# Products with v of two neighbouring groups issued together in a fused attention and MLP kernel

## The chip, the cores and the metric

The kernel runs on one core of one Trainium2 chip. The metric is the device time of one launch in microseconds (us). A comparison of two kernels here can tell them apart from about 0.3% on. TensorE (PE in the rows, its weight loads PEld), VectorE (DVE), ScalarE (ACT), GpSimd (POOL) and SyncE (SP, which issues the DMAs here) run side by side and wait for each other by semaphores.

## The reference

Attention with two kinds of masks over 8 batches, 8 heads, 576 tokens and 64 elements per head, then a token mix of low rank and an MLP with a residual:

```python
scores = q @ k.T / sqrt(64)
# heads 0..3: the last 32 tokens; heads 4..7: every 4th of the last 128
scores = where(mask, scores, -1e9)
attn = softmax(scores)
x = (attn @ v) -> [batch, token, 512]
h = x.T @ U @ V               # rank 32, over the tokens
u = x + h.T
out = u + relu(u @ w_ch1) @ w_ch2     # 512 -> 2048 -> 512
```

## The kernel before, in words

**Attention.** Because of the masks, 64 query rows need only 96 keys. A batch has 18 tiles of 64 query rows by four heads (for heads 4 to 7 the tokens are put in an order in which every 4th token is a neighbour). Two tiles make a **group**, so there are 9 groups per batch (NGB) and 72 in all; a group has four units of two heads each. For a group `score` (L375, L386) makes the scores s, `soften` masks them and takes the exponent (L403 to L410) into the tile p, `turn` (L436, L439; L423 in the early groups) transposes p into one of the buffers `pts`, and `weighted` multiplies it with v (L449) into a PSUM tile pv and divides by the row sums (L453, L454, L479). The sum comes from a column of ones beside v. One group's product with v is 16 matmuls in the trace (8 in the program; each fp32 product is executed as two), with 96 rows and 64 columns of the array in use, where the MLP's have 128 and 128.

**Where the result goes.** For heads 0 to 3, L479 writes x directly. For heads 4 to 7 it writes a tile xp, which from the third batch on has a single buffer, and DMAs (L483) carry its rows to x in the plain token order. Groups 0 to 3 of a batch are of heads 0 to 3 alone, group 4 is half and half, groups 5 to 8 are of heads 4 to 7.

**Token mix.** `split_x`, `t_mm` (L519, tile t) and `mix` (L543, tile m, added to x in L545) do the part with U and V, in 5 pieces of a batch's tokens; one of the 5 has 64 rows, and its matmuls t use 64 rows of the array, the others 128.

**MLP.** Chunks of 384 tokens: `layer1` (L742, tile ph, 12 matmuls for each of 16 columns f) and `layer2` (L759, tile acc, 9 matmuls). For every f, hh (ACT, L747) and hl (DVE, L748) bring ph to SBUF as two halves. The order is layer1(f), layer2(f - 1), so hl of f is read after layer1(f + 1).

**What sets the order.** `batch_items` lists the work of a batch's attention as steps s: `pre` (loads of v and `weighted` of group s - 2, LAG = 2), the four units of group s, and `post` (`turn`). From batch 2 on (SPLIT) each of these has a due time of its own, and the MLP's loop calls what is due between its matmuls (`slot`). Below that, a list scheduler orders the instructions of each engine by its own estimate of time; the order on an engine is fixed at build time. PSUM tiles of the tag "ps" (s, pv, t, m, tp) share three buffers, and the v tiles of the later batches (two per group) three.

Names in the rows: qk, qkr and qks are queries with keys (loaded, split in two halves), vs is V, us is U, w1h, w1l, w2h, w2l the weights' halves.

Of the kernel before, what the change touches and what calls it, by code (L numbers as in the profile page):

```python
# [10 lines left out]
F32 = mybir.dt.float32  # L11
# [15 lines left out]
P = 128  # L27
QB = 64
NJ = S // QB
KB = QB + WIN  # L30
# [10 lines left out]
UNITS = 4  # L41
QK1 = P + KB
DV = D + 1
PV = 2 * DV
# [3 lines left out]
SPLIT = 2  # L48
TILES = [(0, j) for j in range(NJ)] + [(1, NJ - 1)] + [(1, j) for j in range(NJ - 1)]
NGB = len(TILES) // 2  # L50
# [3 lines left out]
LAG = 2  # L54
# [33 lines left out]
F_LAST = 13  # L88
RAWS = 4
VS = 4  # L90
QKS = 9
XPS = 4
DVE_FROM = 2
# [57 lines left out]
def attention_moe_kernel(ctx: ExitStack, tc: tile.TileContext, qk1, qk2, vv, masks, wide, ident, ut, vt, w1, w2, out):  # L151
    nc = tc.nc

    const = ctx.enter_context(tc.tile_pool(name="const", bufs=1))
    work = ctx.enter_context(tc.tile_pool(name="work", bufs=2))
    xpool = ctx.enter_context(tc.tile_pool(name="xpool", bufs=NX))
    dram = ctx.enter_context(tc.tile_pool(name="dram", bufs=2, space=bass.MemoryType.DRAM))
    psum = ctx.enter_context(tc.tile_pool(name="psum", bufs=3, space=bass.MemoryType.PSUM))
# [19 lines left out]
    us = const.tile([P, 9, 2 * RANK], F32R, name="us")  # L178
    vs = const.tile([P, P + S], F32R, name="vs")
    signs = [const.tile([P, DM, 2], F16, name=f"sign{i}") for i in range(NSIGN)]  # L180
    NPT = 2
    pts = [const.tile([KB, UNITS, P], F32, name=f"pt{i}") for i in range(NPT)]
    for p in pts:
        nc.gpsimd.memset(p, 0.0)
# [112 lines left out]
    loaded = {}  # L297
# [7 lines left out]
    def load_v(g, i):  # L305
        if (g, 1, i) not in loaded:
            us_ = slice(2 * i, 2 * i + 2)
            if g < NGB:
                if i == 0:
                    t = xpool.tile([P, UNITS, PV], F32, tag="x", name=f"v{g}")[0:KB]  # L310
                    nc.sync.dma_start(out=t, in_=vv[g])
                    loaded[g, 1, 0] = t[:, 0:2]
                    loaded[g, 1, 1] = t[:, 2:4]
            else:
                t = work.tile([KB, 2, PV], F32, tag="v", name=f"v{g}_{i}", bufs=3)
                nc.sync.dma_start(out=t, in_=vv[g][:, us_])
                loaded[g, 1, i] = t

# [99 lines left out]
    def turn(g, p_sb):  # L418
        pt = pts[g % NPT]
        if g < PE_T:  # L420
# [18 lines left out]
                    nc.vector.transpose(out=pt[ks, :, rs], in_=p_sb[rs, :, ks])  # L439
        return pt  # L440

    def weighted(g, pt):
        b = g // NGB
        pv = psum.tile([P, UNITS, DV], F32, tag="ps", name=f"pv{g}")
        for u in range(UNITS):
            v_sb = loaded[g, 1, u // 2]
            for h in range(2):
                hs = slice(h * DV, (h + 1) * DV)
                nc.tensor.matmul(pv[QB * h:QB * (h + 1), u, :], lhsT=pt[:, u, QB * h:QB * (h + 1)],  # L449
                                 rhs=v_sb[:, u % 2, hs], start=True, stop=True)  # L450
        pool, n_ = (early, 3) if g < NGB else (work, 2)
        ssum = pool.tile([P, UNITS], F32, tag="ssum", name=f"ssum{g}", bufs=n_)
        nc.vector.tensor_scalar(out=ssum, in0=pv[:, :, D], scalar1=1e-9, scalar2=None, op0=ALU.add)  # L453
        nc.vector.reciprocal(out=ssum, in_=ssum)  # L454
        moves = []
        xp = None
        for i in range(2):
            half, j = tile_of(g, 2 * i)
            us_ = slice(2 * i, 2 * i + 2)
            cs = slice(half * HALF_D, (half + 1) * HALF_D)  # L460
            if half == 0:
                t, row = divmod(b * S + j * QB, P)
                dst = x_tile(t)[row:row + QB, cs]
            else:
                if xp is None:
                    if b == 0:
                        xp = early.tile([P, HALF_D], F32, tag="xp", name=f"xp{g}", bufs=XPS)
                    elif b < SPLIT and g % 2:
                        xp = spare[:, 0:HALF_D]
                    else:  # L470
                        xp = work.tile([P, HALF_D], F32, tag="xp", name=f"xp{g}", bufs=1)
                    part = next(p for p, js in enumerate(DPART) if j in js)
                row = QB * DPART[part].index(j)
                dst = xp[row:row + QB]
                moves += [(t, to, n, row + r) for r, t, to, n in runs_of(b, half, j)]
            dst4 = dst.rearrange("p (u h d) -> p u h d", u=2, h=2)
            for h in range(2):
                rs = slice(QB * h, QB * (h + 1))
                nc.vector.tensor_tensor(  # L479
                    out=dst4[:, :, h, :], in0=pv[rs, us_, 0:D],  # L480
                    in1=ssum[rs, us_].unsqueeze(2).broadcast_to([QB, 2, D]), op=ALU.mult)
        for t, to, n, r in sorted(moves):
            nc.sync.dma_start(out=x_tile(t)[to:to + DIL * (n - 1) + 1:DIL, HALF_D:], in_=xp[r:r + n])  # L483
        if moves and b == 0:
            split(b, part, 1, xp, slice(0, QB * len(DPART[part])))
# [96 lines left out]
    def batch_items(b):  # L582
        held = {}
        turned = set()
        attn = []
        for s in range(NGB + LAG):
            g = NGB * b + s

            def pre(s=s, g=g):
                if 0 < s <= NGB:  # L590
                    load_v(g - 1, 0)
                if s >= LAG:
                    weighted(g - LAG, held.pop(g - LAG))
                if b > 0 and 0 < s <= NGB:
                    load_v(g - 1, 1)

            def post(s=s, g=g):
                late = g - (NGB * b < PE_T)
                if late in state and late not in turned:
                    turned.add(late)  # L600
                    held[late] = turn(late, state.pop(late)[0])

            def some(us, g=g):
                for u in us:
                    score(g, u)
                for u in us:
                    n = UNITS * g + u
                    if n >= N2:
                        split_qk(n + LOOK)
                        fetch(n + LOOK + DMA_LOOK)  # L610
                    elif n >= UNITS * NE and n % 2 and n + 2 * TB - 1 < N2:
                        fetch(n + 2 * TB - 1)
                for u in us:
                    soften(g, u)

            step = UNITS if b < SPLIT else STEP
            units = [lambda us=range(u, u + step), some=some: some(us) for u in range(0, UNITS if s < NGB else 0, step)]
            if b < SPLIT:
                attn.append([lambda pre=pre, units=units, post=post: (pre(), [x() for x in units], post())])
            else:  # L620
                attn.append([pre] + units + [post])
        n = len(batch_parts(b))
        after = []
        for c in range(2):
            more = []
            for i in range(n + 1):
                def go(i=i, c=c):
                    if i > 0:
                        t_mm(b, i - 1, c)
                    if i < n and (b, c) != (0, 1):  # L630
                        split_x(b, i, c)
                more.append(go)
            more.append(lambda c=c: t_evict(b, c))
            more += [lambda i=i, c=c: mix(b, i, c) for i in range(n)]
            after.append(more)
        first = NJ // 2 + LAG + 1 + (POST0 if b == 0 else 0)
        per = -(-len(after[0]) // (len(attn) - first))
        if b >= SPLIT:
            timed = []
            for i, step in enumerate(attn):  # L640
                timed += [(i, step[0])] + [(i + UNIT0 + (UNIT1 - UNIT0) * u / len(step[1:-1]), x) for u, x in enumerate(step[1:-1])] + [(i + POST_AT, step[-1])]
                if i >= first:
                    k = (i - first) * per
                    timed += [(i + (m + 0.5) / per, x) for m, x in enumerate(after[0][k:k + per])]
            timed += [(len(attn) + m * TAIL, x) for m, x in enumerate(after[1])]
            end = len(attn) + len(after[1]) * TAIL
            return [(t / end, x) for t, x in sorted(timed, key=lambda e: e[0])]
        items = [x for step in attn[:first] for x in step]
        rest = attn[first:]
        if b == 0:  # L650
            hold = after[0][n + 1:]
            after[0] = after[0][:n + 1]
            m = n + 1
            mixes = [x for p in zip(hold[1:], after[1][m + 1:]) for x in p]
            turns = [lambda t=t: transp(t) for t in range(CT)]
            cut = 2 * CT
            after[1] = [hold[0]] + after[1][:m + 1] + mixes[:cut] + turns + mixes[cut:]
        per = -(-len(after[0]) // len(rest))
        for i, it in enumerate(rest):
            items += it  # L660
            items += after[0][i * per:(i + 1) * per]
        items += after[1]
        return [(i / len(items), x) for i, x in enumerate(items)]
# [60 lines left out]
    for c in range(NCHUNK):  # L724
# [56 lines left out]
        for i in range(CT):  # L781
            t = c * CT + i
# [82 lines left out]
```

## Time and profile before

| | |
|---|---|
| median of 3 runs | 1025.01 us (1024.31 to 1027.09) |
| profiled execution, its own time | 1021.92 us |
| its span in the trace | 1020.1 us |
| PE busy | 982.4 us (96%) in 5904 matmuls |
| DVE busy | 625.1 us (61%) |
| ACT busy | 411.2 us (40%) |
| POOL busy | 324.2 us (32%) |
| share of the chain that ended last: PE | 87% |
| groups' products with v (L449) in that chain | 4% |

The profiled execution is 3.1 us below the median. Busy time of PE is an upper view: matmuls are pipelined, and a row's length overlaps the next one's. What a matmul costs the stream is the step from its start to the next start, and such steps are read from the timeline. The chain of waits tells which engine ended each wait on the path to the last instruction.

### The profile page before, as it was taken

The page shows a single profiled execution, that of the slowest core. Times are in us where ns is not written, and L with a number is a line of the kernel's source. Part 1 is how long each engine was busy: PE and PEld are TensorE (multiplying, and loading weights), DVE is VectorE, ACT ScalarE, POOL GpSimd, SP SyncE. Part 2 cuts the span into 40 slices and gives each one's busy share as a digit, 9 for nine tenths or more (in the row PEclk, how much of TensorE's full clock was granted, in tenths as well). Part 3 has the DMA queues.
Part 4 walks back from the last instruction along what each step waited for, and adds up shares of the span by engine and source line. Part 5 has one row for each costly group of instructions (what it writes and reads, how often), then busy time and mean ns, then how long its engine had stood idle before and what let it go on. Part 6 is the DMA issues. An engine that isn't in the chain of part 4 may idle for free.

```text
span 1020.1 us, 18204 instructions
## 1 busy us (share of the span) xinstructions
PE 982.4 (96%) x5904; PEld 861.3 (84%) x5904; DVE 625.1 (61%) x2155; ACT 411.2 (40%) x986; POOL 324.2 (32%) x519
## 2 busy tenths in 40 slices
PE   7479998999999999999999999999999999999998
PEld 6268886888888888888898888888888888899997
DVE  5978667777368754876457873777647864411211
ACT  3889874343244423445233532434323442111110
POOL 0668673252143421344131621425313431000000
PEclk9579997999999999999999999999999999999999
DMA  9578544243332423333242432434332420400000
GB/s 296 179 238 255 166 143 127 63 129 86 87 88 83 120 73 80 112 111 96 69 107 79 127 81 58 134 83 121 93 80 81 122 61 25 134 1 1 32 1 31
DMA packets 96910, 103.31 MB, mean 101 GB/s; under 512 B 12816, under 2 KB 83536, under 8 KB 96816
## 3 DMA queue, kind: packets, MB, share of 16 engines
q1 hardware_dynamic: 96816, 102.16, 35.0%
q8 instruction: 47, 0.77, 0.3%
q14 instruction: 47, 0.39, 0.1%
HBM read 80.08 MB, written 17.30 MB: 95 GB/s over the span
## 4 chain that ended last, share of the span: by engine, by line
PE 87%; DMA 5%; DVE 3%; ACT 2%; SPq 1%; issue 1%; POOL 0%; DVEq 0%; ACTq 0%; POOLq 0%
PE ph L742 38%; PE acc L759 38%; PE pv L449 4%; PE s L375 3%; PE t L519 2%; PE s L386 1%; DMA zd<-z 1%; DMA raw<-ut 1%; PE m L543 1%; DMA qk<-qk 1%; SPq L483 1%; DMA x<-xp 1%; DMA qkr<-qk 1%; DMA v<-vv 1%; DMA raw<-w 0%
## 5 line engine op out<-in xcount | busy, mean ns | idle before, releaser
L759 PE MATMUL acc<-w2h,hh 128*128 128x512 f32 x576 | 229.0, 398 | 1.1 <-DVE x L784 1.1
L759 PE MATMUL acc<-w2l,hh 128*128 128x512 f32 x576 | 228.0, 396 | 0.0
L352 POOL TENSOR_TENSOR qks<-qkr,qks 128x160 fp32r<-128x160 f32 x192 | 103.6, 539 | 378.5 <-ACT qks L351 238.0
L748 DVE SCALAR_TENSOR_TENSOR hl<-ph,hh 128x384 fp32r<-128x384 f32 x192 | 106.4, 554 | 177.8 <-ACT hh L747 176.5
L759 PE MATMUL acc<-w2h,hl 128*128 128x512 f32 x576 | 210.9, 398 | 0.0
L747 ACT ACTIVATE hh<-ph 128x384 fp32r<-128x384 f32 x192 | 93.8, 488 | 265.0 <-PE ph L742 241.2
L742 PE MATMUL ph<-uth,w1l 128*128 128x384 f32 x768 | 176.2, 341 | 0.0
L742 PE MATMUL ph<-uth,w1h 128*128 128x384 f32 x768 | 173.8, 342 | 0.4 <-ACT uth L579 0.3
L742 PE MATMUL ph<-utl,w1h 128*128 128x384 f32 x768 | 173.0, 339 | 0.0
L410 ACT ACTIVATE p<-p,nmax 128x160 f32<-128x160 f32 (+1 forms) x288 | 111.4, 410 | 122.7 <-DVE nmax L406 119.2
L742 PEld LDWEIGHTS ph<-uth,w1h 128*128 128x128 f32 x768 | 140.1, 190 | 16.7 <-ACT uth L579 1.4
L742 PEld LDWEIGHTS ph<-uth,w1l 128*128 128x128 f32 x768 | 137.4, 190 | 1.1 <-issue 0.4
L742 PEld LDWEIGHTS ph<-utl,w1h 128*128 128x128 f32 x768 | 135.1, 188 | 1.6 <-DVE utl L580 0.2
L351 ACT CAST qks<-qkr 128x288 fp32r<-128x288 f32 x192 | 80.8, 430 | 124.7 <-PE s L375 87.8
L759 PEld LDWEIGHTS acc<-w2h,hl 128*128 128x128 f32 x576 | 107.2, 188 | 23.6 <-issue 0.2
L759 PEld LDWEIGHTS acc<-w2h,hh 128*128 128x128 f32 x576 | 108.2, 188 | 17.5 <-ACT hh L747 1.4
L436 DVE STREAM_TRANSPOSE pt<-p 32x128 f32<-32x128 f32 x384 | 115.6, 301 | 9.5 <-ACT p L410 4.5
L759 PEld LDWEIGHTS acc<-w2l,hh 128*128 128x128 f32 x576 | 108.2, 188 | 15.6
L403 DVE TENSOR_TENSOR p<-s,wide_sb 128x160 f32<-128x160 f32 x192 | 60.3, 320 | 72.4 <-PE s L375 70.7
L355 POOL TENSOR_TENSOR qks<-qkr,qks 64x128 fp32r<-64x128 f32 x192 | 90.7, 473 | 15.1
L499 POOL TENSOR_TENSOR xhl<-x,xhl 128x256 fp32r<-128x256 f32 (+1 forms) x70 | 51.6, 759 | 87.7 <-ACT xhl L497 55.1
L406 DVE CUSTOM_DVE_ANT_0 p<-s,p 128x160 f32<-128x160 f32 x192 | 60.3, 320 | 3.7
(67 smaller groups left out, 965.3 us busy)
## 6 DMA issues: line engine op xcount, KB each, us to landing
qkr<-qk SPq DMA_DIRECT2D x192, 144.0 KB, 2.2
raw<-w SPq DMA_DIRECT2D x26, 512.0 KB, 4.7
v<-vv SPq DMA_DIRECT2D x126, 97.5 KB, 2.0
out<-x SPq DMA_DIRECT2D x36, 256.0 KB, 2.2
zd<-z SPq DMA_DIRECT2D x120, 64.0 KB, 2.0
xt<-zd SPq DMA_DIRECT2D x30, 256.0 KB, 2.8
qk<-qk SPq DMA_DIRECT2D x9, 448.0 KB, 7.8
qkr<-qk SPq DMA_DIRECT2D x18, 224.0 KB, 3.9
```

The source lines that it names most:

```text
L351: nc.scalar.copy(out=t[:, 0:QK2], in_=raw)
L352: nc.gpsimd.tensor_tensor(out=t[:, QK2:], in0=raw[:, P:], in1=t[:, P:QK2].bitcast(F32), op=ALU.subtract)
L355: eng.tensor_tensor(out=t[lo, 0:P], in0=raw[lo, 0:P], in1=t[lo, 0:P].bitcast(F32), op=ALU.subtract)
L403: nc.vector.tensor_tensor(out=p_sb[:, u, :], in0=sp[:, 0:KW], in1=wide_sb[:, kind], op=ALU.add)
L406: nc.vector.tensor_tensor_reduce(out=p_sb[rs, u, 0:w], in0=a, in1=c, scale=-1.0 / 8.0, scalar=3.0e38, op0=ALU.add, op1=ALU.min, accum_out= ...
L410: nc.scalar.activation(out=p_sb[:, u, 0:w], in_=p_sb[:, u, 0:w], func=AF.Exp, bias=nmax[:, u:u + 1], scale=-1.0,)
L436: nc.vector.transpose(out=to[:, :, WIN * (r % 2):WIN * (r % 2 + 1)], in_=p_sb[rs, :, QB * s + WIN * k:QB * s + WIN * (k + 1)])
L499: eng.tensor_tensor(out=xl[rs], in0=x[rs], in1=xh[rs].bitcast(F32), op=ALU.subtract)
L742: nc.tensor.matmul(ph, lhsT=w[:, k, :], rhs=u[:, k, :], start=(n == 0), stop=(n == len(seq) - 1))
L747: nc.scalar.activation(out=hh, in_=ph, func=AF.Relu)
L748: nc.vector.scalar_tensor_tensor(out=hl, in0=ph, scalar=0.0, in1=hh.bitcast(F32), op0=ALU.max, op1=ALU.subtract)
L759: nc.tensor.matmul(acc[i], lhsT=h[:, ss], rhs=w, start=(f == 0 and n == 0), stop=(f == FC - 1 and n == 2))
```

## The change

`weighted` takes a list of groups: first all matmuls with v of the groups, each into a pv tile of its own, then the division of each (`normalize`, the same instructions as before). From batch 2 on it is called in every second step with two groups, 0 and 1, 2 and 3, 4 and 5, 6 and 7, and in the last step with group 8: 5 calls per batch where there were 9. Batches 0 and 1 call it with one group as before. The buffers for transposed probabilities become three for the whole kernel (one more is zeroed by POOL at the start), and the v tiles of the later batches get four buffers for three.

```diff
--- before.py
+++ after.py
@@ -88,6 +88,7 @@
 F_LAST = 13
 RAWS = 4
 VS = 4
+VBUF = 4
 QKS = 9
 XPS = 4
 DVE_FROM = 2
@@ -178,7 +179,7 @@
     us = const.tile([P, 9, 2 * RANK], F32R, name="us")
     vs = const.tile([P, P + S], F32R, name="vs")
     signs = [const.tile([P, DM, 2], F16, name=f"sign{i}") for i in range(NSIGN)]
-    NPT = 2
+    NPT = 3
     pts = [const.tile([KB, UNITS, P], F32, name=f"pt{i}") for i in range(NPT)]
     for p in pts:
         nc.gpsimd.memset(p, 0.0)
@@ -312,7 +313,7 @@
                     loaded[g, 1, 0] = t[:, 0:2]
                     loaded[g, 1, 1] = t[:, 2:4]
             else:
-                t = work.tile([KB, 2, PV], F32, tag="v", name=f"v{g}_{i}", bufs=3)
+                t = work.tile([KB, 2, PV], F32, tag="v", name=f"v{g}_{i}", bufs=VBUF)
                 nc.sync.dma_start(out=t, in_=vv[g][:, us_])
                 loaded[g, 1, i] = t
 
@@ -439,15 +440,22 @@
                     nc.vector.transpose(out=pt[ks, :, rs], in_=p_sb[rs, :, ks])
         return pt
 
-    def weighted(g, pt):
+    def weighted(gs):
+        pvs = []
+        for g, pt in gs:
+            pv = psum.tile([P, UNITS, DV], F32, tag="ps", name=f"pv{g}")
+            pvs.append((g, pv))
+            for u in range(UNITS):
+                v_sb = loaded[g, 1, u // 2]
+                for h in range(2):
+                    hs = slice(h * DV, (h + 1) * DV)
+                    nc.tensor.matmul(pv[QB * h:QB * (h + 1), u, :], lhsT=pt[:, u, QB * h:QB * (h + 1)],
+                                     rhs=v_sb[:, u % 2, hs], start=True, stop=True)
+        for g, pv in pvs:
+            normalize(g, pv)
+
+    def normalize(g, pv):
         b = g // NGB
-        pv = psum.tile([P, UNITS, DV], F32, tag="ps", name=f"pv{g}")
-        for u in range(UNITS):
-            v_sb = loaded[g, 1, u // 2]
-            for h in range(2):
-                hs = slice(h * DV, (h + 1) * DV)
-                nc.tensor.matmul(pv[QB * h:QB * (h + 1), u, :], lhsT=pt[:, u, QB * h:QB * (h + 1)],
-                                 rhs=v_sb[:, u % 2, hs], start=True, stop=True)
         pool, n_ = (early, 3) if g < NGB else (work, 2)
         ssum = pool.tile([P, UNITS], F32, tag="ssum", name=f"ssum{g}", bufs=n_)
         nc.vector.tensor_scalar(out=ssum, in0=pv[:, :, D], scalar1=1e-9, scalar2=None, op0=ALU.add)
@@ -589,8 +597,8 @@
             def pre(s=s, g=g):
                 if 0 < s <= NGB:
                     load_v(g - 1, 0)
-                if s >= LAG:
-                    weighted(g - LAG, held.pop(g - LAG))
+                if s >= LAG and (b < SPLIT or (s - LAG) % 2 or s == NGB + LAG - 1):
+                    weighted([(k, held.pop(k)) for k in sorted(held) if k <= g - LAG])
                 if b > 0 and 0 < s <= NGB:
                     load_v(g - 1, 1)
 
```

How the instructions stand on the engines, at three places (names: pv36 is the product of group 36, which is group 0 of batch 4; the number behind the last underscore tells tiles apart and means nothing; a matmul row here is executed as two where its inputs are fp32).

PE at the first pair of batch 4, before:

```order
L759 MATMUL acc4_0_4995<-w2h_0_86,hh4_1_5067 128x512
L449 MATMUL pv36_5101<-v36_0_5003,pt0_77 64x65 x4
L449 MATMUL pv36_5101<-v36_1_5005,pt0_77 64x65 x4
L375 MATMUL s38_0_5139<-qks152_5054 128x320
L759 MATMUL acc4_0_4995<-w2l_0_87,hh4_1_5067 128x512
...
L759 MATMUL acc4_2_4997<-w2l_0_87,hh4_2_5133 128x512
L449 MATMUL pv37_5219<-v37_0_5099,pt1_78 64x65 x4
L449 MATMUL pv37_5219<-v37_1_5118,pt1_78 64x65 x4
L759 MATMUL acc4_2_4997<-w2h_0_86,hl4_2_5134 128x512
```

and with the change:

```order
L767 MATMUL acc4_2_4999<-w2h_0_88,hl4_2_5119 128x512
L750 MATMUL ph4_4_5262<-uth4_4935,w1h_0_86 128x384 x4
L452 MATMUL pv36_5204<-v36_0_5005,pt0_77 64x65 x4
L452 MATMUL pv36_5204<-v36_1_5007,pt0_77 64x65 x4
L452 MATMUL pv37_5213<-v37_0_5101,pt1_78 64x65 x4
L452 MATMUL pv37_5213<-v37_1_5103,pt1_78 64x65 x4
L376 MATMUL s39_0_5251<-qks156_5154 128x320
L750 MATMUL ph4_4_5262<-uth4_4935,w1l_0_87 128x384 x4
```

The two groups' products stand without a row between them. All 24 pairs of batches 2 to 7 do, so their products are 30 runs in PE's order where they were 54.

PE at the token mix of batch 4, pieces 3 and 4 of the first half (piece 4 is the one of 64 rows), before:

```order
L449 MATMUL pv42_5803<-v42_0_5662,pt0_77 64x65 x4
L449 MATMUL pv42_5803<-v42_1_5685,pt0_77 64x65 x4
L519 MATMUL t4_0_5751<-xhl4_3_0_5836,us_73 64x256 x2
L519 MATMUL t4_0_5751<-xhl4_4_0_5902,us_73 64x256 x2
L759 MATMUL acc4_1_4996<-w2h_6_802,hl4_12_5980 128x512
```

and with the change:

```order
L376 MATMUL s44_1_5849<-qks177_5766 128x320
L527 MATMUL t4_0_5753<-xhl4_3_0_5815,us_73 64x256
L527 MATMUL t4_0_5753<-xhl4_4_0_5881,us_73 64x256
L750 MATMUL ph4_15_6087<-uth4_4935,w1h_13_1461 128x384 x3
L750 MATMUL ph4_15_6087<-uth4_4935,w1l_13_1462 128x384 x3
L527 MATMUL t4_0_5753<-xhl4_4_0_5881,us_73 64x256
L750 MATMUL ph4_15_6087<-uth4_4935,w1l_13_1462 128x384
```

The two matmuls of the piece of 64 rows stood together and now stand apart, here and in batches 2 and 6: runs of such matmuls in batches 2 to 7 go from 18 to 21.

DVE at the pair of groups 6 and 7 of batch 3 (33 and 34), both of which write the single buffer xp, before:

```order
L479 TENSOR_TENSOR xp33_4360<-pv33_4348,ssum33_4357 64x2x64 x4
L406 ISA p35_4386,nmax35_4387<-s35_1_4407,p35_4386 128x160
...
L748 SCALAR_TENSOR_TENSOR hl3_6_4593<-ph3_6_4579,hh3_6_4592 128x384
...
L453 TENSOR_SCALAR ssum34_4484<-pv34_4475 128x4
L454 RECIPROCAL ssum34_4484<-ssum34_4484 128x4
L479 TENSOR_TENSOR xp34_4487<-pv34_4475,ssum34_4484 64x2x64 x4
```

and with the change:

```order
L487 TENSOR_TENSOR xp33_4476<-pv33_4455,ssum33_4473 64x2x64 x4
L553 TENSOR_TENSOR x14_3759<-x14_3759,m3_1_0_4547 128x256
L756 SCALAR_TENSOR_TENSOR hl3_9_4714<-ph3_9_4700,hh3_9_4713 128x384
L487 TENSOR_TENSOR xp34_4489<-pv34_4464,ssum34_4486 64x2x64 x4
L461 TENSOR_SCALAR ssum35_4562<-pv35_4553 128x4
L462 RECIPROCAL ssum35_4562<-ssum35_4562 128x4
```

The second group's division came behind a softmax and now follows the first one's with two instructions between them; it waits until the DMAs have read xp33.

## Rows read from the trace of the kernel before

**Rows 1.** Busy time by stretch (us), instructions in brackets; clock, DMA share, GB/s.

```profile
36.00:43.00 7.00, 4.55 (x53) 3.62 (x53) 6.85 (x14) 6.36 (x13) 7.00 (x7) 0.50 0.53 164
410.00:530.00 120.00, 120.00 (x730) 106.00 (x729) 80.72 (x293) 44.98 (x113) 41.37 (x78) 1.00 0.36 99
530.00:650.00 120.00, 118.86 (x722) 104.36 (x721) 81.49 (x288) 47.52 (x116) 40.75 (x76) 1.00 0.34 90
```

**Rows 2.** What PE waited for from 190 us on: total, times, longest.

```profile
PE acc L759 <- DVE x L784: 1.1, 1, 1.1
PE ph L742 <- ACT uth L579: 0.3, 1, 0.3
```

**Rows 3.** Timeline of PE, batch 4: start, length, instructions merged, count.

```profile
422.94 0.39 PE L759 MATMUL acc<-w2h,hh 128*128 128x512 f32 x1
423.18 0.40 PE L759 MATMUL acc<-w2l,hh 128*128 128x512 f32 x1
423.50 0.69 PE L449 MATMUL pv<-v,pt 96*64 96x65 f32 x16
424.12 0.50 PE L759 MATMUL acc<-w2h,hl 128*128 128x512 f32 x1
424.45 0.86 PE L742 MATMUL ph<-uth,w1h 128*128 128x384 f32 x4
...
427.29 0.39 PE L759 MATMUL acc<-w2h,hl 128*128 128x512 f32 x1
```

**Rows 4.** Timeline of PE, the group before that one.

```profile
415.93 0.40 PE L759 MATMUL acc<-w2h,hh 128*128 128x512 f32 x1
416.26 0.69 PE L449 MATMUL pv<-v,pt 96*64 96x65 f32 x16
416.87 0.42 PE L375 MATMUL s<-qks 128*128 128x320 f32 x1
417.13 0.39 PE L759 MATMUL acc<-w2l,hh 128*128 128x512 f32 x1
```

**Rows 5.** Timeline of PE in batch 0: two groups in a row, then one.

```profile
36.45 2.00 PE L449 MATMUL pv<-v,pt 96*64 96x65 f32 x32
...
41.75 1.14 PE L449 MATMUL pv<-v,pt 96*64 96x65 f32 x16 [2.40 <-issue]
```

**Rows 6.** Groups by line: busy us, mean ns of one; idle before, releaser.

```profile
L449 PE MATMUL pv<-v,pt 96*64 96x65 f32 x1152 | 50.5, 232 | 2.4 <-issue 2.4
L479 DVE TENSOR_TENSOR xp<-pv,ssum 64x128 f32<-64x128 f32 x134 | 38.6, 288 | 7.5 <-DMA x<-xp 4.8
L184 POOL MEMSET pt<- 96x512 f32 x2 | 1.0, 522 | 0.3 <-POOLq L856 0.3
```

**Rows 7.** Timeline of PE around one matmul t of 64 rows.

```profile
262.18 0.40 PE L759 MATMUL acc<-w2l,hh 128*128 128x512 f32 x1
262.51 0.33 PE L519 MATMUL t<-xhl,us 64*64 64x256 f32 x1
262.77 0.50 PE L759 MATMUL acc<-w2h,hl 128*128 128x512 f32 x1
263.10 0.40 PE L759 MATMUL acc<-w2h,hh 128*128 128x512 f32 x1
```

**Rows 8.** Timeline of PE around one matmul t of 128 rows.

```profile
156.24 0.40 PE L759 MATMUL acc<-w2l,hh 128*128 128x512 f32 x1
156.47 0.28 PE L519 MATMUL t<-xhl,us 128*64 128x256 f32 x1
156.59 0.39 PE L759 MATMUL acc<-w2h,hl 128*128 128x512 f32 x1
```

**Rows 9.** Timeline of PE, start of the MLP: the last wait before a closed stream.

```profile
73.03 0.69 PE L386 MATMUL s<-qkr 128*128 128x96 f32 x4 [1.22 <-DMA qkr<-qk]
```

**Rows 10.** Line L483: ns min/median/max of an issue on SP's queue.

```profile
L483 SPq DMA_DIRECT2D x<-xp x180: 469/582/1725, 30.0 to 853.6; - x180
```

**Rows 11.** DMA issues: count, KB each, median us from issue to landing.

```profile
x<-xp SPq DMA_DIRECT2D x88, 32.0 KB, 1.9
```

**Rows 12.** Timeline of DVE: the hl that PE reads first at 427.29.

```profile
422.04 0.56 DVE L748 SCALAR_TENSOR_TENSOR hl<-ph,hh 128x384 fp32r<-128x384 f32 x1 [1.04 <-ACT hh L747]
```

## The prediction, made before the change was run

> **What bounds the kernel now.** I read the busy time by stretch first. In batch 4 PE is busy for all 120.00 us of a 120.00 us stretch at the full granted clock, DVE for 80.72 us; the next stretch looks the same but for 1.1 us [rows 1]. The waits of PE say the same from the other side: from 190 us on it waits 1.4 us in all [rows 2]. So from the third batch on PE's stream of matmuls is closed, and what shortens the stream shortens the kernel; what the other engines do costs nothing as long as it is not late for a matmul. A busy row of PE doesn't tell whether its matmuls run at their best step, so I read the timeline next, from start to start.
>
> Two acc matmuls ahead of a group's product start 0.24 us apart (422.94, 423.18). From the second to the product's first matmul it takes 0.32 us, the product lasts 0.62 us up to the next acc's start, and from there to the next ph it is 0.33 us [rows 3]. So the stream pays beside the product itself: about 0.09 us before it, and 0.10 us after the first matmul behind it. From 423.18 to 424.45 are 1.27 us; two acc steps of 0.235 us (0.23 us apart in [rows 8], 0.24 in [rows 3]) are 0.47, so **one group's product costs the stream 0.80 us**. The group before it gives the same picture with an s behind it: 1.20 us from 415.93 to 417.13 [rows 4], less 0.235 for the acc and 0.147 for the s (an estimate: 320 of 512 columns of an acc step) is 0.82 us. I take 0.81.
>
> **What a second group costs in the same run.** The trace has one such case, in batch 0, where the granted clock is 0.50 [rows 1], that is 1.2 GHz: 32 matmuls take 2.00 us and 16 take 1.14 us, so the second group adds 0.86 us and no edge [rows 5]. At 2.4 GHz it is at best half of that, 0.43 us. From the other side: 16 matmuls span 0.69 us [rows 3], the last is 0.23 us long [rows 6], so 15 steps take 0.46 us, and 16 of them 0.49, which still has the longer first step of a run in it. I take 0.46, the middle.
>
> **The change, part by part.** 1. 24 pairs become one run each (groups 0 to 7 of six batches; group 8 stays alone). Each saves 0.81 - 0.46 = 0.35 us: 24 x 0.35 = **8.4 us less**. The ends are 0.80 - 0.49 = 0.31 and 0.82 - 0.43 = 0.39, so 7.4 to 9.4 us.
>
> 2. The new order takes apart three pairs of t matmuls of 64 rows (18 runs become 21). Such a matmul alone takes 262.18 to 263.10, 0.92 us with two acc, so 0.45 us [rows 7]; of that 0.12 us is the step of a t that pays no edge (156.47 to 156.59, [rows 8]) and is paid anyway. 3 x 0.33 = **1.0 us more**.
>
> 3. The divisions on DVE are the same instructions, one group's behind the other's. The even group's comes a step later, group 8's stays where it was, so the batch's end doesn't move. DVE has 39 us of 120 free [rows 1]. What is new is a wait: groups 4 and 5, and 6 and 7, write the single buffer xp one after the other, and the second write waits for DMAs. Cost on the path: 0, hidden by the time that hl has in hand: the hl of 422.04 is done at 422.60 [rows 12] and first read at 427.29 [rows 3], 4.7 us later. Behind the waiting division stand the next hl, for PE, and softmaxes, for ACT and later groups' products. What it costs if that cover goes is the first rival.
>
> 4. Four v buffers for three: the same DMAs. The next pair's v starts when the pair is done and is needed two steps later; two groups were 7.2 us apart even where they stood close (416.26, 423.50, [rows 3, 4]), and transfers of this queue land in some 2 us [rows 11], so SP's waits stay beside the stream. If they didn't, the queries and keys queued behind them would be late for s. The third buffer of transposed probabilities keeps `turn` as free as it was; POOL zeroes 0.52 us more at the start [rows 6], before its other work.
>
> 5. The scheduler also moves rows of the first 75 us, where PE isn't closed: an early v load before the weights, the last four mix matmuls of batch 0 behind the first ph. The trace can't price this; the last wait before the stream closes, 1.22 us [rows 9], may go or double, and with the zeroing I bound it by 1.7 us to either side and take 0.
>
> **Sum.** -8.4 + 1.0 = -7.4 us. The profiled execution took 1021.92 us, so it would take 1014.5. It lies 3.1 us under the median of the runs shown, for which I forecast 1025.01 - 7.4 = **1017.6 us**.
>
> **A rule weighed against the rows.** The rows show that the edge hangs on the rows used: a t of 128 rows and 64 columns starts 0.23 us after an acc and is followed after 0.12 us [rows 8], no edge, while one of 64 rows and 64 columns pays it on both sides [rows 7], as the product with 96 rows does. The Trainium skill, TensorEngine Tiling (Array Packing), section Key Properties, says that changing the tiling mode, not merely the tile, drains the TensorE; it lists 128 by 64 as a mode of its own. By that, every run of t would pay the edge too; for the product with v the rows agree, for the t of 128 rows they don't, and the rows decide. By the rule the sum would be 5.6 us for 7.4 (the last rival).
>
> **Rivals.** Late hl, slower than before. The division that waits for xp waits for the DMAs that read it, five after group 33: 5 x 0.58 us of issues [rows 10] and 1.9 us of landing [rows 11], 4.8 us. Between the two divisions of groups 33 and 34 DVE now has an addition and an hl of 0.56 us [rows 12], so up to 4.2 us of standing; behind it come four multiplications of 0.29 us [rows 6] and the next hl, 0.56: 5.9 us against the 4.7 in hand, so PE would wait 1.2 us in each of 12 pairs, 14.4 us: 1032.0. It eats the gain from 0.6 us per pair on, and makes the kernel measurably slower from 0.87 us on. For it: the two instructions in between. Against it: the addition waits for a mix matmul that stands behind the pair and 24 MLP matmuls on PE, which gives the DMAs their time unseen, and in all of the run before DVE lost only 4.8 us to such waits [rows 6], none of which PE felt [rows 2]. Chance 0.03.
>
> No run. The second group's matmuls wait for their own transposed probabilities or PSUM buffer, or pay the edge again: nothing is saved and 1.0 us is added, 1026.0. Against it: [rows 5], and the operands are a step old by then. Chance 0.06.
>
> PSUM. A pair holds two of the three buffers that s, t and m also use, and the next s stands still until DVE has divided. Half of the saving of a pair lost, 24 x 0.17 = 4.1 us: 1021.7. Against it: PE's order puts only one s or m right behind a pair and then a whole ph or acc group, and DVE needs 1.5 us for a division. Chance 0.07.
>
> Every run of 64 columns pays the edge. Counting t of 128 rows in, runs with 64 columns go from 103 to 87, because t is taken apart more often: 16 x 0.35 = 5.6 us, 1019.4. Against it: [rows 8]. Chance 0.04. This is the case of the skill's rule above.
>
> **How the numbers follow.** My own case has 0.80. Its bounds are 6.4 to 8.4 us of gain, with 1.7 us to either side: 1014.9 to 1020.3. The range reaches up to the PSUM case, and 0.4 us below, for runs that differ by more than that: 1014.5 to 1021.9; it leaves out the first two rivals and little else. A measurement of this kernel can tell about 0.3%, 3.1 us, from no change, so faster means under 1021.9: 0.85, from my case, the last rival and most of the PSUM case. Within 0.3%: 0.11, from the case without a saving and the tail of the others. Slower: 0.04.
>
> **What would show it.** Right: in the timeline of PE rows of 32 matmuls of about 1.15 us in batches 2 to 7, 24 of them, with the next matmul 1.08 us after the first; as many PE waits from 190 us on as before; the MLP's end some 7 us earlier relative to its start. DVE's waits for the DMAs of xp may grow, to some 20 us, without a PE wait from hl. Wrong: acc waiting for hl (the first rival); runs of 16 with a pause between them, or a gap at the seam as long as at an edge (the second); s or m waiting for DVE's division (the third); t of 128 rows with an edge (the last). A start of the closed stream that is more than 1.7 us off would be the part that I could not price.

## The result, and the profile after

The changed kernel takes **1031.87 us** in the median of six runs (1029.17 to 1036.3), the kernel before beside it 1024.98 us (1024.31 to 1027.09): a ratio of 1.0070, 95% interval 1.0050 to 1.0091. It is slower by 7 us, where 7.4 us less was forecast. The profiled executions say the same: 1029.17 us for 1021.92 us.

What PE waits for from 190 us on is the first view to read, as in [rows 2]:

```profile
PE ph L750 <- ACT uth L587: 9.9, 3, 3.6
PE acc L767 <- DVE hl L756: 0.8, 2, 0.4
```

The 0.3 us that stood there for ph and uth have become 9.9 us, in three waits of over 3 us. The wait that I had feared, acc for hl, is there with 0.8 us. The stretches say where; these answer to [rows 1]:

```profile
410.00:530.00 120.00, 119.52 (x731) 106.16 (x730) 79.04 (x288) 44.91 (x113) 38.81 (x74) 1.00 0.33 93
530.00:650.00 120.00, 116.88 (x709) 103.67 (x708) 81.59 (x288) 45.98 (x112) 39.03 (x74) 0.98 0.33 94
```

The second stretch loses 3.1 us of PE, and its clock is 0.98 for 1.00. Inside it, the timeline of PE shows one hole:

```profile
642.24 0.86 PE L767 MATMUL acc<-w2h,hl 128*128 128x512 f32 x3
642.93 0.31 PE L376 MATMUL s<-qks 128*128 128x320 f32 x1
646.37 0.69 PE L750 MATMUL ph<-uth,w1h 128*128 128x384 f32 x1 [3.12 <-ACT uth L587]
```

From the s to the ph it takes 3.43 us instead of 0.15. This ph is the first of MLP chunk 7. The last 192 of the chunk's 384 tokens are the first of batch 5, and they are complete only when that batch's attention and token mix are. The same hole stands before the first ph of chunk 4 (403.24 to 406.80) and of chunk 10 (883.04 to 886.99), which hold the first tokens of batches 3 and 7. Busy time in short stretches shows what follows a hole (columns as in [rows 1]; the number behind POOL's bracket is the clock):

```profile
639.00:643.00 4.00, 4.00 (x20) 3.21 (x18) 2.54 (x9) 1.22 (x4) 1.00 (x2) 1.00 0.62 171
643.00:646.00 3.00, 0.24 (x2) 0.00 (x0) 3.00 (x7) 1.38 (x5) 2.21 (x4) 0.87 0.57 157
646.00:649.00 3.00, 2.63 (x8) 2.63 (x9) 2.54 (x10) 1.06 (x3) 0.98 (x2) 0.50 0.70 192
649.00:652.00 3.00, 3.00 (x11) 3.00 (x11) 0.00 (x0) 0.00 (x0) 0.00 (x0) 0.50 0.94 320
652.00:655.00 3.00, 2.95 (x16) 2.52 (x15) 2.76 (x13) 2.80 (x8) 2.00 (x4) 0.99 0.14 41
```

PE had waited for 3.12 us, and for the next 6 us it runs at 1.2 GHz. At half the clock these 6 us do 3 us of work, so this pause costs nearly twice its length. Behind the pauses at 403.24 and 883.04 the clock is down for a shorter time.

What was meant to happen did happen. A pair is one row of 32 matmuls, and the next matmul starts 1.08 us after its first:

```profile
364.28 1.15 PE L452 MATMUL pv<-v,pt 96*64 96x65 f32 x32
365.36 0.39 PE L551 MATMUL m<-ts,vs 128*128 128x256 f32 x1
```

A single group takes 0.62 us there [rows 3], so the second one costs 0.46 us, as forecast.

**Where the chain got longer.** The waits before the divisions into xp have grown. This is the row that answers to [rows 6]:

```profile
L487 DVE TENSOR_TENSOR xp<-pv,ssum 64x128 f32<-64x128 f32 x134 | 38.7, 288 | 29.8 <-DMA x<-xp 27.5
```

27.5 us for 4.8. The timeline of DVE at the end of batch 5 shows the three last divisions of the batch, those of groups 6, 7 and 8, first before the change:

```profile
598.31 1.21 DVE L479 TENSOR_TENSOR xp<-pv,ssum 64x128 f32<-64x128 f32 x4
...
604.50 1.22 DVE L479 TENSOR_TENSOR xp<-pv,ssum 64x128 f32<-64x128 f32 x4
...
612.08 1.21 DVE L479 TENSOR_TENSOR xp<-pv,ssum 64x128 f32<-64x128 f32 x4
```

and after it:

```profile
608.00 1.21 DVE L487 TENSOR_TENSOR xp<-pv,ssum 64x128 f32<-64x128 f32 x4
...
612.93 1.22 DVE L487 TENSOR_TENSOR xp<-pv,ssum 64x128 f32<-64x128 f32 x4 [1.62 <-DMA x<-xp]
...
619.25 1.21 DVE L487 TENSOR_TENSOR xp<-pv,ssum 64x128 f32<-64x128 f32 x4 [2.07 <-DMA x<-xp]
```

Before, the three stand 6 to 8 us apart because their products do, and each finds xp free. After, group 6 comes with group 7 (a pair at 603.9), and the three stand 4.9 and 6.3 us apart because xp is one buffer: a division, five or six DMA issues of 0.58 us [rows 10], a landing of 1.9 us [rows 11], the next division. SP's queue at the end of batch 3 shows this cycle:

```profile
368.97 4.16 SPq L491 DMA_DIRECT2D x<-xp  x5
373.23 0.52 SPq L317 DMA_DIRECT2D v<-vv  x1
375.11 3.68 SPq L491 DMA_DIRECT2D x<-xp  x6
378.88 0.53 SPq L317 DMA_DIRECT2D v<-vv  x1
380.80 3.04 SPq L491 DMA_DIRECT2D x<-xp  x5
```

What counts is the last one. Group 8's product starts at 610.23 before and at 611.60 after. These two rows are that product, before and after:

```profile
610.23 0.69 PE L449 MATMUL pv<-v,pt 96*64 96x65 f32 x16
```

```profile
611.60 0.69 PE L452 MATMUL pv<-v,pt 96*64 96x65 f32 x16
```

Its division ends 3.06 us later before (612.08 + 1.21) and 8.86 us later after (619.25 + 1.21). From there the second half of the token mix, the turned rows and uth follow. The last uth of chunk 7 before:

```profile
639.48 0.62 ACT L579 CAST uth<-xt 128x512 fp32r<-128x512 f32 x1 [0.34 <-DMA xt<-zd]
```

and after:

```profile
645.70 0.62 ACT L587 CAST uth<-xt 128x512 fp32r<-128x512 f32 x1 [1.62 <-DMA xt<-zd]
```

So the **chain** from the start of group 8's product to the end of the chunk's last uth is 640.10 - 610.23 = 29.87 us before and 646.32 - 611.60 = 34.72 us after. PE's own **work** between that product and the chunk's first ph is 641.04 - 610.23 = 30.81 us before (it comes 0.94 us after uth is there) and 31.48 us after (up to the s of 642.93 and its step of 0.15). The chain is 3.24 us longer than the work, and that is the pause.

The other two chunks, worked out in the same way. At chunk 10 the division goes from 3.1 to 8.5 us, the chain from 30.0 to 34.5 and the work from 29.5 to 30.8. At chunk 4 the division goes from 3.1 to 9.4 us, but the chain only from 34.4 to 34.8, while the work falls from 34.5 to 31.4. The chain looks long there before the change because the casts to uth wait for their turn: they follow, with no wait of their own, a p that waited for DVE.

```profile
402.75 0.43 ACT L410 ACTIVATE p<-p,nmax 128x160 f32<-128x160 f32 x1 [3.97 <-DVE nmax L406]
403.09 1.65 ACT L579 CAST uth<-xt 128x512 fp32r<-128x512 f32 x3
```

So at chunk 4 two things meet: the late division, and an order in which PE has 3 us less to do between group 8's product and the chunk's first ph.

### The profile page after: what moved, and what is told of

Its sections match the earlier page's. It is cut to its first block, busy times and chain, and to the rows that moved or that the text cites. A ratio compares the mean times of both kernels' runs of the same rounds, so it can differ in the third digit from the quotient of the medians.

```text
span 1027.4 us, 18181 instructions
## 1 busy us (share of the span) xinstructions
PE 981.1 (95%) x5904; PEld 865.6 (84%) x5904; DVE 630.8 (61%) x2155; ACT 409.9 (40%) x986; POOL 323.4 (31%) x520
## 3 DMA queue, kind: packets, MB, share of 16 engines
q1 hardware_dynamic: 96816, 102.16, 34.2%
## 4 chain that ended last, share of the span: by engine, by line
PE 86%; DVE 5%; ACT 4%; DMA 3%; issue 1%; SPq 1%; POOL 0%; DVEq 0%; ACTq 0%
PE ph L750 38%; PE acc L767 38%; PE pv L452 3%; PE s L376 3%; PE t L527 2%; PE s L387 1%; PE m L551 1%; DMA qk<-qk 1%; DMA xt<-zd 1%; ACT sign L210 1%; DMA mask<-masks 1%; DVE v L217 1%; ACT v L209 1%; ACT sign L211 1%; ACT p L411 0%
## 5 line engine op out<-in xcount | busy, mean ns | idle before, releaser
L750 PE MATMUL ph<-uth,w1h 128*128 128x384 f32 x768 | 178.0, 346 | 10.3 <-ACT uth L587 10.3
L750 PEld LDWEIGHTS ph<-uth,w1l 128*128 128x128 f32 x768 | 139.7, 192 | 1.1
```

The source lines that it names most:

```text
L750: nc.tensor.matmul(ph, lhsT=w[:, k, :], rhs=u[:, k, :], start=(n == 0), stop=(n == len(seq) - 1))
```

## The experiments

Theories A to D and A2 are told in the expectations. Ratios are to the kernel before, run beside each on the same chip, with 95% intervals.

The edits also change the order that the scheduler gives PE, and in some kernels it takes pairs apart again. Counted in PE's timeline as rows of 32 matmuls, all 24 pairs stand unbroken in the changed kernel, but 21 of 24 in experiment 1, 5 of 6 with groups 6 and 7 alone, 17 of 18 in the kernel of three pairs with two buffers xp, 20 of 24 with a buffer for group 8's division alone, and 17 of 18 without the pair 4 and 5; in the others all stand. Only one of the broken pairs that write xp lies at the end of a batch before chunk 4, 7 or 10: groups 6 and 7 of batch 5 in the kernel that pairs these alone, where the two products start 2.2 us apart (602.65 and 604.86).

**1. Two buffers for xp.** Only this differs from the changed kernel:

```diff
-    xp = work.tile([P, HALF_D], F32, tag="xp", name=f"xp{g}", bufs=1)
+    xp = work.tile([P, HALF_D], F32, tag="xp", name=f"xp{g}", bufs=2)
```

> The changed kernel with two buffers xp for one. Theory A (the single xp puts the last three divisions of a batch one behind the other, so the second half of the token mix and the transposed rows come too late for chunks 4, 7 and 10): the three pauses of 3.4 to 4.0 us at the starts of these chunks shrink to under 1.5 us each, the clock stays at 1.0 behind them, DVE's waits for the DMAs of xp fall from 27.5 us to under 10, and the time falls from 1031.9 to 1016 to 1022 us. Theory B (what delays the rows is that the even group's division comes a step later, whatever its buffer): pauses and half clock stay, 1029 to 1032 us. Theory C (the loads of v, queued on SP with four buffers, push the other DMAs back): as B, 1029 to 1032 us.

Measured: 1018.52 us, ratio 0.9962 (0.9948 to 0.9977). PE's waits from 190 us on:

```profile
PE acc L767 <- DVE x L792: 1.3, 1, 1.3
PE s L376 <- DVE nmax L407: 1.2, 1, 1.2
PE acc L767 <- ACT hh L755: 0.6, 1, 0.6
PE s L376 <- DVE x L487: 0.6, 1, 0.6
PE ph L750 <- DVE utl L588: 0.5, 1, 0.5
```

The three waits for uth are gone, and by the ratios 11 us with them; DVE's waits for the DMAs of xp are 1.5 us. B and C fall. Others are left, 4.2 us in all, spread over different places, so the full saving of the pairs isn't reached. That these waits are the reason was not tested.

**2. Only pairs that don't touch xp** (groups 0 with 1, 2 with 3):

```diff
-    if s >= LAG and (b < SPLIT or (s - LAG) % 2 or s == NGB + LAG - 1):
+    if s >= LAG and (b < SPLIT or s - LAG in (1, 3, 4, 5, 6, 7, 8)):
```

> The changed kernel, but only groups 0 with 1 and 2 with 3 of each batch from the third on are issued together; groups 4 to 8, which write xp, go alone as before: 12 pairs instead of 24. Theory A: no pair touches xp, so no pause over 1.5 us at chunks 4, 7 and 10; the 12 pairs save 12 x 0.35 = 4.2 us: 1019 to 1023 us. Theory B: the end of the batch is as in the kernel before, so the same 1019 to 1023 us; it is the first kernel of this series that parts A from B, this one parts both from C and from pairs that save nothing. Theory C: four v buffers and three of transposed probabilities are still there, so the pauses stay: 1028 us and more. If pairs saved nothing: 1025 us.

Measured: 1017.95 us, ratio 0.9941 (0.9917 to 0.9964): half of the pairs, and 6 us less than before, more than the 1019 to 1023 us that A and B expected. No wait for uth. The four v buffers are still there, so C falls; part of the gain is that of experiment 3.

**3. No pairs, but the other buffers and the order that these give:**

```diff
-    if s >= LAG and (b < SPLIT or (s - LAG) % 2 or s == NGB + LAG - 1):
+    if s >= LAG:
```

> The changed kernel with no group paired: only the fourth v buffer, the third buffer of transposed probabilities and the order that these give. Theories A and B: no pauses at chunks 4, 7 and 10, as many runs of 64 columns as before, so 1023 to 1027 us. Theory C: pauses of over 2 us at these chunks, 1030 us or more. The start (first ph, 63.9 us in the kernel before and 65.0 in the changed one) tells whether the zeroing of the third buffer costs it: then 65 here.

Measured: 1020.73 us, ratio 0.9975 (0.9960 to 0.9990). No pauses, so C falls here too. The gain of 1 to 4 us was expected by no theory; I did not find its cause, and the expectations below that count from it are loose by as much.

**4. The kernel before with two buffers xp** (the edit of 1, in the kernel before).

> The kernel before, with two buffers xp for one, as a control: its three pauses over 1 us (647.7, 878.0, 256.3: 2.6 us in all) and its 4.8 us of DVE waits for the DMAs of xp are small, so theories A, B and C all give no change that can be measured, 1022 to 1026 us; a gain of over 3 us would mean that the buffer bound the kernel before already, and that its gain in the changed kernel says nothing on the pairs.

Measured: 1022.87 us, ratio 0.9993 (0.9974 to 1.0012). Without pairs the second buffer is worth nothing.

**5 to 8. Which pairs?** The edit is that of 2 with another list of steps: (0, 1, 2, 3, 4, 5, 7, 8) for groups 6 and 7 alone,

> Of the four pairs of a batch only groups 6 and 7 go together; all else of the changed kernel stands. Theory A (single xp: divisions of 6, 7 and 8 one behind the other): the pauses at chunks 4, 7 and 10 are there in full, 2.5 to 4 us each, with the half clock behind them, and only 6 pairs save 0.34 us each: slower than the kernel beside it by 5 to 13 us, no better than the changed kernel. Theory D (the rows are no later than before; PE is only ahead by what pairs 0 to 3 saved, and gives that back in a pause): with 2 us saved in all the pauses are under 1 us each and the time is within 3 us of the kernel before. Theory A expects DVE waits of over 2 us before the xp divisions of groups 7 and 8.

(0, 1, 2, 3, 5, 6, 7, 8) for groups 4 and 5 alone,

> Only groups 4 and 5 go together. They write xp too, but what needs their rows comes later than with groups 6 to 8. Theory A in the form that only the batch's last divisions count: no pause over 1.5 us at chunks 4, 7 and 10, and 6 x 0.34 = 2.1 us less than the kernel without pairs (which was 2.5 us under the kernel before): 3 to 6 us faster than before. Theory A in the form that any wait for xp counts: pauses as with groups 6 and 7, 1 to 8 us slower than before.

(1, 3, 5, 6, 7, 8) for the pairs 0 and 1, 2 and 3, 4 and 5,

> Pairs of groups 0 and 1, 2 and 3, 4 and 5; groups 6, 7 and 8 alone, one xp. Theory A (last divisions): 18 x 0.34 = 6.2 us less, no pause over 1.5 us: 5 to 8 us faster than before. Theory D: PE is ahead by more than with two pairs, so the pauses come back, 1 us or less faster.

and the same with two buffers xp.

> As the kernel with three pairs, with two buffers xp. Theory A: what is left of DVE's waits for the DMAs of xp goes, and what PE lost by them: the same as with one buffer or up to 2 us less, 6 to 9 us faster than before; if the best version, then because groups 6, 7 and 8 are divided each as soon as it is there. If pairing costs through a late even group rather than through xp, the same time as with one buffer.

Measured, in this order: 1022.37 us, ratio 0.9977 (0.9962 to 0.9991); 1021.83 us, 0.9974 (0.9955 to 0.9992); 1019.85 us, 0.9956 (0.9943 to 0.9970); 1017.81 us, 0.9931 (0.9915 to 0.9947). The second has no pause at the three chunk starts, but gains only 2.7 us (by the interval 0.8 to 4.6) where A expected 3 to 6. Its profiled execution, 2.4 us above its median, starts the first ph 3.3 us late (67.23 for 63.88); whether the other executions do, and whether that is the reason, isn't shown. The third and the fourth gain 4.5 us (A expected 5 to 8) and 7.1 us by the ratios, where D wanted the pauses back. **The first is a miss for A**: groups 6 and 7 alone make the kernel no slower, although at the end of batch 5 DVE waits 2.00 and 1.52 us before the divisions of groups 7 and 8 there too, and the division of group 8 ends 7.1 to 8.7 us after its product's start at the three places. In that kernel the chain at chunk 7 is 33.36 us, as long as a late division makes it, but PE's order holds 33.89 us of work beside it; at chunk 4 it is 33.80 us beside 32.87, and there is a pause of 1.0 us. So the late division is not enough by itself; it needs too little work beside it. That is theory A2, and the order of PE gives the work before a kernel runs.

**9 to 11. Chain against work.** First all four pairs again, with a buffer for group 8's division alone:

```diff
-    xp = work.tile([P, HALF_D], F32, tag="xp", name=f"xp{g}", bufs=1)
+    xp = work.tile([P, HALF_D], F32, tag="xq" if g % NGB == 8 else "xp", name=f"xp{g}", bufs=1)
```

> All four pairs of the changed kernel; group 8 alone has a buffer xp of its own, groups 4 to 7 share the one. Theory A2: a pause at chunks 4, 7 and 10 is the length of the chain (group 8's product to its last division, then mix, turned rows, uth) less PE's work from that product to the chunk's first ph (31.9, 31.9 and 31.4 us here by counting its matmuls at 0.175, 0.233, 0.146 and 0.12 us; 30.3, 30.3 and 29.7 in the changed kernel). Group 8 no longer waits for group 7's DMAs, so product to last division falls from some 8 us to some 4, the chain from 34.6 to about 30.5 us, under PE's work: no pause over 1.2 us there, and 3 to 6 us faster than the kernel before. Theory D (PE is ahead by the pairs' saving, whatever the buffer): pauses of over 2 us, slower than before.

Measured: **1016.61 us, ratio 0.9915 (0.9885 to 0.9946)**, the best median of the series, with 20 of the 24 pairs unbroken and all four in the batches before chunks 4, 7 and 10. The gain is above the 3 to 6 us that A2 expected. Of DVE's waits for xp 19.1 us are still there, but not before the last division (timeline of DVE, end of batch 5), and PE waits 1.0 us in all:

```profile
604.92 1.22 DVE L487 TENSOR_TENSOR xp<-pv,ssum 64x128 f32<-64x128 f32 x4
...
609.91 1.21 DVE L487 TENSOR_TENSOR xp<-pv,ssum 64x128 f32<-64x128 f32 x4 [2.33 <-DMA x<-xp]
...
611.90 1.21 DVE L487 TENSOR_TENSOR xp<-pv,ssum 64x128 f32<-64x128 f32 x4
```

```profile
PE acc L767 <- DVE x L792: 0.6, 2, 0.3
PE acc L767 <- DVE hl L756: 0.4, 2, 0.2
```

The chain is 32.06 us at chunk 7, longer than the 30.5 expected, and the work 33.08. The new order thus has 1.6 us more work beside the chain than the changed kernel (31.48); against that kernel's work a pause of 0.6 us would be left. Next, groups 4 and 5 alone and the other three pairs, steps (1, 3, 4, 5, 7, 8), one xp:

> Pairs of groups 0 and 1, 2 and 3, 6 and 7; groups 4 and 5 alone, one xp. The order of PE leaves unequal work between group 8's product and the first ph of the chunk: 34.0 us at chunk 4, 28.3 at chunk 7, 30.8 at chunk 10. Theory A2, with a chain of 33 to 34.6 us: no pause over 1.2 us at chunk 4, 4.5 to 6.5 us at chunk 7, 2 to 4 us at chunk 10; with the half clock behind them within 4 us of the kernel before. Theory D: three pauses that are alike, 2 to 3 us each.

Measured: 1028.68 us, ratio 1.0033 (1.0014 to 1.0052). The three chunk starts in the timeline of PE:

```profile
402.85 0.31 PE L376 MATMUL s<-qks 128*128 128x320 f32 x1
403.00 0.87 PE L750 MATMUL ph<-uth,w1h 128*128 128x384 f32 x4
...
639.67 0.60 PE L376 MATMUL s<-qks 128*128 128x320 f32 x3
645.04 1.65 PE L750 MATMUL ph<-uth,w1h 128*128 128x384 f32 x4 [4.77 <-ACT uth L587]
...
882.19 0.86 PE L767 MATMUL acc<-w2h,hl 128*128 128x512 f32 x3
884.89 0.96 PE L750 MATMUL ph<-uth,w1h 128*128 128x384 f32 x4 [1.84 <-ACT uth L587]
```

No pause, one of 4.8 us, one of 1.8 us (PE's waits, in brackets): three unequal ones in one kernel, in the order and near the sizes that the work beside the chain foretold. The work itself measures 35.1, 29.5 and 32.1 us, 1.1 to 1.3 us more than was counted from the order, and the chain 34.0, 34.4 and 34.1. D wanted three alike. Then the pairs that touch xp without the others, steps (0, 1, 2, 3, 5, 7, 8):

> Pairs of groups 4 and 5 and of 6 and 7; groups 0 to 3 and 8 alone, one xp: the half of the pairs that touch xp. PE's work from group 8's product to the chunk's first ph is 32.5, 33.1 and 32.9 us. Theory A2, with a chain of 33 to 34.6 us: pauses of 0 to 2 us each, 12 x 0.34 = 4.1 us saved: within 0 to 5 us under the kernel before. If pairs 4 with 5 and 6 with 7 together made the loss whatever the work beside them: pauses of over 3 us each, slower than before.

Measured: 1019.91 us, ratio 0.9954 (0.9928 to 0.9980), no pause at these chunks, though DVE waits 31.5 us for the DMAs of xp, more than in the changed kernel.

**12. The pairs of 2 with two buffers xp.**

> Only pairs of groups 0 and 1, 2 and 3, with two buffers xp: whether the second buffer adds to the best kernels so far (these two pairs with one buffer 0.9941 of before, three pairs with two buffers 0.9931). Theory A2: with groups 6, 7 and 8 alone the chain is 30 to 31.6 us against 31.9 of work, so the second buffer gives nothing: 4 to 8 us faster than before, the same as with one.

Measured: 1017.98 us, ratio 0.9937 (0.9913 to 0.9960), as with one buffer.

Chunk 7 in nine kernels, in us, each worked out from starts and ends in the timelines as above (division: from group 8's product to the end of its division; the chain contains it):

| kernel | division | chain | work | pause |
|---|---|---|---|---|
| before | 3.1 | 29.9 | 30.8 | 0 |
| **changed** | 8.9 | 34.7 | 31.5 | **3.2** |
| two xp | 2.9 | 30.5 | 30.9 | 0 |
| group 8 its own buffer | 4.2 | 32.1 | 33.1 | 0 |
| only 6 with 7 | 8.2 | 33.4 | 33.9 | 0 |
| only 4 with 5 | 4.3 | 30.1 | 30.9 | 0 |
| all but 6 with 7 | 7.0 | 31.0 | 31.5 | 0 |
| all but 4 with 5 | 8.1 | 34.4 | 29.5 | **4.9** |
| 4 with 5, 6 with 7 | 9.7 | 33.9 | 34.2 | 0 |

That a pause stands exactly where the chain is longer than the work follows from how the columns are worked out, since the ph starts when both are done; the test was experiment 11, where the order of PE gave the pauses before the run. What the table shows is where the two lengths come from. That the chain is longer comes, at chunk 7, from the division's column: what is left of it behind the division is 24.0 to 27.9 us in all nine, and the shortest of it belongs to kernels whose division is late, so a part of the delay is caught up. The work differs by up to 4.7 us from order to order, and a division of 9.7 us makes no pause beside 34.2 us of work.

## Why the prediction was wrong

**Part 1, the pairs, held.** 0.46 us for the second group in a run, as forecast, beside 0.62 from a single group's first matmul to the next row, as before. With group 8's buffer apart the kernel is 8.5 us faster than before (1016.61 for 1025.16; by the interval 5.5 to 11.8), where the sum had 7.4. That is no clean measure of the pairs: 20 of 24 stand unbroken there, and 2.6 us less (1 to 4) came in experiment 3 without any pair. What is left, some 6 us, is what 20 pairs at 0.35 us less the 1.0 us of the t matmuls give. Part 2, the t matmuls taken apart, was not tried by itself. The other rivals are not seen: the second group's matmuls follow without a gap or an edge (1.08 us for the pair), no s or m waits for DVE's division in PE's waits from 190 us on, and a t of 128 rows still starts 0.23 us after an acc and is followed after 0.12 us in the changed kernel (506.90, 507.13, 507.25).

**Part 3 failed**, in the words "group 8's stays where it was, so the batch's end doesn't move", and in the cover that it named. At chunks 7 and 10 the product of group 8 stayed within 1.3 us of its place before the chunk, and at chunk 4 it came 3 us nearer to it; its division came late at all three. The cost on the path, put at 0, came out as 10.4 us of pauses and at most 6.1 us of slower clock behind them (the sum below). I counted the waits for xp from group 6 to group 7 and not on from 7 to 8, and what I put against them was hl with 4.7 us in hand. hl had them, but for 0.8 us of PE's waits. But the same division also heads the chain to the next chunks' uth, and this chain had 0.94 us in hand at chunk 7 and none at chunk 10; at chunk 4 what it had was used up by the new order as well. The trace of before said so: the second of [rows 2], ph waiting 0.3 us for uth, is the chunk 10 start of that kernel. I read it as nothing because it was small. A small wait at the end of a long chain says that the chain has no room; 5.8 us more in it (8.86 less 3.06) had to come out at PE, less what the rest of the chain caught up (26.81 us before, 25.86 after) and what work the new order puts beside it.

The first rival had the right wait and the wrong victim. It made hl late, in each of twelve pairs, and gave 1032.0 us; the time came out at 1031.87 by another way, three pauses and the clock behind them. That the two figures agree is chance. Its chance of 0.03 was weighed for hl alone.

**Part 4 held** (experiment 3: no pauses with the four v buffers). **Part 5** stayed inside its 1.7 us: the first ph starts at 65.03 for 63.88 us. Over the other kernels this start lies between 63.9 and 67.2 us, so it adds about that much looseness to every comparison.

**The sum, by the profiled executions.** Pairs -8.2 (24 x 0.343, with 0.467 for the second group), t +1.0 as forecast, start +1.1, the three pauses +10.4 (3.56 + 3.43 + 3.95 less a normal step each), the half clock behind them at most +6.1 (1 less the clock, times the length, over the stretches of 3 us behind each), the waits for hl +0.8, less the 1.4 us of waits that stood in the kernel before [rows 2]: 9.8 us slower, measured 7.25. The clock's share is an upper bound, since PE also stands in some of these stretches; what else makes up the 2.6 us is open. Experiment 3's unexplained gain is as large, but that it is the same isn't shown.

The Trainium skill, TensorE: Matmul & The Clock Gate, section HAM oscillation, describes how a matmul stream that waits for DMAs falls back to the slower clock and pays for it after each wait. The rows agree: 0.50 from 646 to 652 us, behind a wait for DMAs by way of xp, zd and uth.

The Trainium skill, Trainium Kernel Development and Optimization, section Best Practices, says to double-buffer so that DMA and compute overlap. The runs agree with a limit: a second xp takes 11 us from the kernel with pairs (by the ratios 1.0070 and 0.9962) and nothing from the one without (1022.87 for 1023.29), where the products stand some 7 us apart (596.38, 603.29 and 610.23 at the end of batch 5) and one buffer is enough.

## What to carry to other kernels

When work is batched, the member that waits for its partner is late, and so is everything that shares a buffer behind it; follow that buffer to the last user of the stage, and compare the chain behind that user with the work beside it. Look for a chain's room in its smallest wait, not in its largest: a wait of 0.3 us at the end of a chain of 30 us says that there is none. Even so the wait told of one of the three places only; at the other two, chain and work had to be compared. A second buffer kept for the batch's last group did at least as much as one shared by all (1016.61 and 1018.52 us, on different chips and with other orders of PE), and the total of DVE's waits told nothing: with 27.5 us of them there were three pauses, with 31.5 us none at these places.

## What was not expected of the hardware

How long the clock stays down differs from pause to pause. Behind the 3.43 us at 642.93 it was 0.50 for 6 us; behind the 3.56 us at 403.24 it was 0.55 from 407 to 410 and 1.00 after that:

```profile
403.00:407.00 4.00, 0.75 (x4) 0.39 (x3) 3.60 (x8) 2.38 (x6) 2.46 (x5) 0.91 0.67 179
407.00:410.00 3.00, 3.00 (x11) 3.00 (x12) 2.28 (x9) 0.75 (x2) 0.80 (x2) 0.55 0.88 288
410.00:413.00 3.00, 3.00 (x18) 2.72 (x16) 1.62 (x9) 1.61 (x5) 0.96 (x2) 1.00 0.71 212
```

A shorter pause is followed by the lower clock too: in the kernel without the pair 4 and 5 PE waits 1.84 us for uth before the ph of 884.89, and the clock is 0.64 in the next 3 us:

```profile
882.00:885.00 3.00, 1.16 (x6) 0.63 (x5) 1.63 (x4) 0.62 (x1) 0.00 (x0) 1.00 0.62 175
885.00:888.00 3.00, 3.00 (x12) 3.00 (x13) 2.17 (x4) 0.00 (x0) 0.00 (x0) 0.64 0.67 208
888.00:891.00 3.00, 3.00 (x14) 2.80 (x14) 0.24 (x1) 0.56 (x2) 0.00 (x0) 0.79 0.97 255
```

Not every pause of about that length is followed by it: in the kernel with the pairs 4 with 5 and 6 with 7, PE waits 1.65 us for DVE before the acc of 648.86, and the clock stays at 1.00 behind it:

```profile
649.00:652.00 3.00, 2.81 (x11) 1.70 (x12) 3.00 (x12) 0.85 (x2) 0.99 (x2) 1.00 0.81 279
```
